# A diffusion transformer block on one core: scale/K weights in 4+5 tiles, ones in PSUM, early transposes, another LN1 order

## The chip, the cores and the metric

One core of one Trainium2 chip. The metric is the device time of one execution in microseconds (us). In the text PE is TensorE, DVE VectorE, ACT ScalarE, POOL GpSimd and SP SyncE, which issues the weight loads and the output stores. SBUF is the on-chip memory that loads go to, PSUM the one that PE writes its sums to. A DMA "lands" when its data have arrived. The "dense part" is the stretch from the first K matmul on, where PE hardly ever waits.

## The reference, cut to what matters

```python
B, N, D = (2, 256, 1152)                      # F = 4 * D, all bfloat16
mod = (_silu(c) @ w_mod).reshape(B, 6, 1, D)
shift_a, scale_a, gate_a, shift_m, scale_m, gate_m = [mod[:, i] for i in range(6)]
h = _layernorm(x, axis=-1) * (1 + scale_a) + shift_a
qkv = (h @ wqkv).reshape(B, N, 3, H, Dh)      # H = 2
# ... attention, wo, gate, second layernorm, gelu MLP
return x + gate_m * m
```

## The kernel before

D is nine tiles of 128 ("k-tiles"); the 512 tokens are four token tiles, two a batch. The program is a list of units with dependencies; a small list scheduler fixes each engine's order ahead of time, and PE's order is simply the order of the source. K needs only LN(x)·(1+scale), since the shift adds the same vector to every key row's product and is put in for Q and V later. So the kernel loads the scale columns of w_mod and the K weights first and starts K as soon as the first columns are there:

```python
KC = 5                                        # k-tiles in the first scale part
for (ka, kb) in ((0, KC), (KC, KT)):          # loads: scale part, its K weights, next part ...
    for k0 in range(0, KT, 3):                # a part comes in three thirds
        dma(WSC[:, k0:k0 + 3, ka * P:kb * P], wmod_v[:, k0:k0 + 3, D + ka * P:D + kb * P], ...)
    for kt in range(ka, kb):
        dma(WK[:, kt, :], wqkv_v[:, kt, D:2 * D], ...)
for k0 in range(0, KT, 3):                    # then the shift weights
    dma(WSH[:, k0:k0 + 3, :], wmod_v[:, k0:k0 + 3, 0:D], ...)

def ln_stats_act(src, junk, mv_t, msq, rstd_t, tag):      # token tiles 0 and 3
    act(... Square, accum_out=msq ...)
    act(... Identity, scale=1.0 / D, accum_out=mean ...)
    dve(... var = mean * mean - msq ...)
    dve(... var = -var + EPS ...)
    pool(... rstd = var ** -0.5 ...)

def sc1a(ka, kb):                             # 1 + scale, PSUM to SBUF
    dve(... tensor_scalar(out=o, in0=m, scalar1=1.0, op0=ALU.add) ...)

# PE's order
warm(7, "b"); ...                             # warm-up matmuls on zeros
xn_T(1)                                       # transposes of a normalised token tile
# scale sums of k-tiles 0-2, xn_T(0), sums 3-5, warm, sums 6-8, warm
sc1a(0, KC)
for kt in range(KC): hk(kt, 0, ...)           # HK = xn * (1 + scale)
for kt in range(KC):
    for i in range(4): k_pair((kt,), i, 0)    # K, batch 0, two output tiles a pair
    if kt == 1: xn_T(2)
    if kt == 2: xn_T(3)
k_pair(range(KC), 0, 1)                       # K, batch 1
for kt in range(KT): mod_kt(WSC, kt, 0, ..., (KC, KT))   # second scale part, 36 small matmuls
sc1a(KC, KT)
k_pair(range(KC), 1, 1); k_pair(range(KC), 2, 1)         # 20 matmuls hide the copy
# ... rest of K
S.unit("pe", KT * c_mm(CH) + 100.0, "shr")    # "the shift product": reads WSH k-tile by k-tile
# ...
k_pair(range(KT), 3, 1, bank=1)               # the last K pair, 18 matmuls
# ... then Q, attention, V, wo, MLP
```

## Time and profile before

| before | |
|---|---|
| median of 3 runs | 247.52 us (247.26 to 247.64) |
| span of the profiled run | 245.2 us |
| PE busy | 98% |
| last first-part scale third has landed | 10.93 us |
| first K matmul | 12.28 us |
| last PE matmul starts | 242.39 us |
| last store issued | 243.38 us |

The landings are the times at which the last of a DMA's 16 semaphore increments came; the first K matmul is the first one with 256 columns.

First lines of the page of before: the span, PE's and the weight loads' busy time, the share of the 40 slices in which PE was busy, the clock that the throttle granted, and the chain that ended last.

```profile
span 245.2 us, 4025 instructions
PE 240.2 (98%) x1750; PEld 147.6 (60%) x1760; DVE 98.5 (40%) x201; ACT 63.1 (26%) x127; POOL 20.2 (8%) x34
...
PE   7999999999999999999999999999999999999995
...
PEclk9999999999999999999999999999999999999999
...
PE 94%; DMA 3%; SPq 1%; DVE 0%; issue 0%
```

PE is the engine that the time is made of: nearly the whole chain runs through it, at full granted clock. "Busy" in the first slices includes warm-up matmuls that compute nothing, so those slices are not full of work.

The same chain in order of time, of before: start, length, what.

```profile
2.82 8.11 DMA arena<-in_w_mod_dram
10.93 0.05 issue
10.97 0.67 PE psum L687 x15
11.64 0.02 issue
11.66 0.18 DVE arena L788
11.85 0.03 issue
11.87 0.36 DVE arena L797
12.23 0.04 issue
12.28 1.92 PE psum L687 x16
14.20 0.50 PE psum L690 x9
...
16.08 16.11 PE psum L687 x198
```

Read downwards: a scale load, 15 scale sums, "1+" (line 788), the first scaling (line 797), K. From 12.28 us on it is PE alone. The start costs 1.35 us from the landing to K.

PE in order of time around the second scale sums (first line) and around the shift product (second line), of before; a bracket with an idle time would stand at the end of a line if PE had waited.

```profile
16.79 5.46 PE L687 MATMUL psum<-arena 128*128 128x256 bf16 x74
26.77 3.46 PE L687 MATMUL psum<-arena 128*128 128x256 bf16 x51
```

No bracket: PE ran through both places. Taken matmul by matmul there were two short gaps, 0.06 us after the matmul that starts at 17.55 and 0.13 us after that at 18.48.

### The profile page before, as it was taken

What the parts mean: (1) busy time and instruction counts of PE and PEld (TensorE: products, weight loads), DVE (VectorE), ACT (ScalarE), POOL (GpSimd) and SP (SyncE); (2) the same over time, 40 slices, a digit from 0 to 9 for tenths busy, and PEclk for the clock granted to TensorE, in tenths of its full rate; (3) what the DMA queues carried; (4) which work ended last, traced back from release to release, by engine and by line L of the source; (5) the groups of instructions that cost most, each with busy time, mean ns of one, the idle gap of its engine ahead of it and who ended that gap; (6) DMA issues with size and microseconds to landing.
All of it is one profiled execution on the core that took longest, in us unless ns stands there. A gap on an engine that the chain in (4) does not pass through costs nothing.

```text
span 245.2 us, 4025 instructions
## 1 busy us (share of the span) xinstructions
PE 240.2 (98%) x1750; PEld 147.6 (60%) x1760; DVE 98.5 (40%) x201; ACT 63.1 (26%) x127; POOL 20.2 (8%) x34
## 2 busy tenths in 40 slices
PE   7999999999999999999999999999999999999995
PEld 2588754457666766798544444444556655665675
DVE  3743450456312679869999700000012222111112
ACT  5730340244312305983322233222000000000000
POOL 1300000000011166600000000020000000000000
PEclk9999999999999999999999999999999999999999
DMA  6999999999993999969943589003000000000000
GB/s 236 364 377 392 391 390 407 417 422 404 382 305 112 340 387 391 391 211 402 349 122 111 182 268 357 0 3 96 0 16 19 16 16 20 16 16 16 29 22 19
DMA packets 28844, 51.59 MB, mean 210 GB/s; under 512 B 1559, under 2 KB 15643, under 8 KB 28827
## 3 DMA queue, kind: packets, MB, share of 16 engines
q1 hardware_dynamic: 28384, 50.14, 56.7%
q0 software_dynamic: 416, 1.19, 1.5%
q8 instruction: 14, 0.23, 0.4%
q14 instruction: 3, 0.02, 0.0%
q10 hardware_dynamic: 27, 0.00, 0.0%
HBM read 50.14 MB, written 1.19 MB: 209 GB/s over the span
## 4 chain that ended last, share of the span: by engine, by line
PE 94%; DMA 3%; SPq 1%; DVE 0%; issue 0%
PE psum L687 92%; DMA arena<-in_w_mod_dram 3%; PE psum L690 2%; SPq L668 1%; DVE arena L797 0%; DVE arena L1214 0%; DVE arena L1215 0%; DVE arena L788 0%
## 5 line engine op out<-in xcount | busy, mean ns | idle before, releaser
L687 PE MATMUL psum<-arena 128*128 128x384 bf16 (+12 forms) x1661 | 236.7, 310 | 2.4 <-POOL arena L710 1.4
L687 PEld LDWEIGHTS psum<-arena 128*128 128x128 bf16 (+3 forms) x1671 | 142.2, 97 | 92.5 <-issue 4.6
L1214 DVE TENSOR_TENSOR arena<-psum,arena 128x384 f32<-128x384 f32 (+3 forms) x14 | 7.0, 501 | 68.0 <-PE psum L687 68.0
L1124 ACT ACTIVATE arena<-psum 128x512 bf16<-128x512 f32 (+1 forms) x44 | 22.4, 520 | 42.7 <-PE psum L687 42.7
L684 DVE CAST arena<-psum 128x512 bf16<-128x512 f32 (+4 forms) x22 | 13.8, 633 | 31.7 <-PE psum L687 31.6
L682 ACT ACTIVATE arena<-psum 128x512 bf16<-128x512 f32 (+6 forms) x27 | 14.7, 562 | 35.0 <-PE psum L687 32.4
L1025 DVE SCALAR_TENSOR_TENSOR arena<-arena 128x1152 f32<-128x1152 bf16 x16 | 22.7, 1416 | 0.5
L1092 POOL TENSOR_TENSOR arena<-arena 128x384 f32<-128x384 f32 x12 | 10.9, 911 | 14.0 <-DVE arena L1091 11.8
L668 POOL DMA_DIRECT2D dit_scratch<-arena x3 | 1.8, 610 | 116.7 <-ACT arena L682 59.9
L734 DVE BATCH_NORM_STATS2 arena<-arena 128x6 f32<-128x384 f32 (+1 forms) x18 | 9.5, 549 | 0.0
L1037 DVE CAST arena<-psum 72x32 bf16<-72x32 f32 x1 | 0.2, 188 | 21.2 <-PE psum L687 21.2
L1091 DVE TENSOR_TENSOR arena<-psum,arena 128x384 f32<-128x384 f32 x12 | 6.7, 555 | 3.8 <-PE psum L687 3.8
L1097 ACT ACTIVATE arena<-arena 128x1152 bf16<-128x1152 f32 x4 | 5.3, 1344 | 9.8 <-DVE arena L1096 9.8
L690 PEld LDWEIGHTS psum<-arena 128*128 128x128 bf16 (+1 forms) x89 | 5.8, 98 | 2.4 <-DMA arena<-in_c_dram 0.8
L1215 DVE TENSOR_TENSOR arena<-arena 128x384 bf16<-128x384 f32 (+3 forms) x14 | 7.0, 502 | 0.5
L690 PE MATMUL psum<-arena 128*128 128x128 bf16 (+1 forms) x89 | 7.1, 219 | 0.1
L1114 ACT ACTIVATE arena<-psum,arena 128x128 bf16<-128x128 bf16 x16 | 6.1, 455 | 2.8 <-PE psum L690 2.2
L1111 DVE TENSOR_SCALAR arena<-psum,arena 128x128 bf16<-128x128 bf16 x20 | 5.5, 337 | 1.9 <-PE psum L690 1.9
L955 ACT ACTIVATE arena<-psum,arena 128x256 bf16<-128x256 f32 x8 | 3.7, 469 | 7.3 <-DVE arena L952 4.6
L738 POOL TENSOR_TENSOR arena<-arena 128x1 f32<-128x1 f32 x6 | 3.3, 552 | 7.9 <-DVE arena L737 7.9
L951 DVE TENSOR_REDUCE arena<-psum 128x2 f32<-128x512 f32 x4 | 2.8, 692 | 2.6 <-PE psum L687 2.6
L797 DVE TENSOR_SCALAR arena<-psum,arena 128x256 bf16<-128x256 bf16 x7 | 2.4, 349 | 3.6 <-PE psum L690 2.3
(43 smaller groups left out, 42.9 us busy)
## 6 DMA issues: line engine op xcount, KB each, us to landing
arena<-in_w_mod_dram SPq DMA_DIRECT2D x4, 2592.0 KB, 20.2
arena<-in_w_fc_dram SPq DMA_DIRECT2D x9, 1152.0 KB, 7.3
arena<-in_w_fc_dram SPq DMA_DIRECT2D x4, 2592.0 KB, 16.2
arena<-in_wqkv_dram SPq DMA_DIRECT2D x18, 288.0 KB, 9.9
arena<-in_w_mod_dram SPq DMA_DIRECT2D x3, 864.0 KB, 12.5
arena<-in_wqkv_dram SPq DMA_DIRECT2D x1, 2592.0 KB, 12.1
arena<-in_wo_dram SPq DMA_DIRECT2D x1, 2592.0 KB, 32.8
arena<-in_w_mod_dram SPq DMA_DIRECT2D x3, 480.0 KB, 7.5
```

Of the source, the lines that this page charges most:

```text
L682: act(c_act(n), lambda e: e.activation(out=dst, in_=src, func=ACTF.Copy), [src], [dst], name)
L684: dve(c_dve_psum16(n) if psum16 else c_dve_psum32(n), lambda e: e.tensor_copy(dst, src), [src], [dst], name)
L687: S.instr(lambda e: e.matmul(o, lhsT=l, rhs=r, start=st, stop=sp, **kw), reads=[l, r], writes=[o])
L690: S.instr(lambda e: e.transpose(o, i_, idn), reads=[i_, idn], writes=[o])
L734: dve(550, lambda e, s=s, o=o: e.bn_stats(out=o, in_=s), [s], [o], "bn_%s_%d" % (tag, ci))
L1025: dve(1270, lambda e, w=w, s=s, acc=acc: e.scalar_tensor_tensor(out=acc, in0=w, scalar=s, in1=acc, op0=ALU.mult, op1=ALU.add), [w, s, acc] ...
L1091: dve(550, lambda e, o=o, ga=ga, x1c=x1c: e.tensor_tensor(out=x1c, in0=o, in1=ga, op=ALU.mult), [o, ga], [x1c], "wo_t1_%d_%d" % (t, ci))
L1092: S.op("pool", 930, lambda e, xs=xs, x1c=x1c: e.tensor_tensor(out=x1c, in0=x1c, in1=xs, op=ALU.add), reads=[x1c, xs], writes=[x1c], name=" ...
L1114: act(440, lambda e, o=o, dst=dst, s1=s1, s2=s2: e.activation(out=dst, in_=o, func=ACTF.Identity, scale=s1, bias=s2), [o, s1, s2], [dst], ...
L1124: act(c_act(ntok), lambda e: e.activation(out=dst, in_=o, func=ACTF.Gelu_apprx_tanh), [o], [dst], "gelu_%d_%d" % (f, tok0))
L1214: dve(c_dve_psum32(w), lambda e, o=o, gm=gm, t1=t1: e.tensor_tensor(out=t1, in0=o, in1=gm, op=ALU.mult), [o, gm], [t1], "fc2_t1_%d_%d" % ( ...
L1215: dve(c_dve_32(w), lambda e, t1=t1, x1c=x1c, ost=ost: e.tensor_tensor(out=ost, in0=t1, in1=x1c, op=ALU.add), [t1, x1c], [ost], "fc2_out_%d ...
```

## The change

The intent: start K earlier (a smaller first scale part, a shorter chain from its sums to K), put work into the time in which PE waits anyway (transposes of token tile 3), and rearrange what was tight. The core of the diff:

```diff
-KC = 5
+KC = 4
@@ LN1 statistics on ACT (token tiles 0 and 3)
-            act(... Square ...);  act(... Identity, mean ...)
-            dve(... var = mean * mean - msq ...);  dve(... -var + EPS ...)
+            act(... Identity, mean ...)
+            pool(... var = mean * mean - EPS ...)
+            act(... Square ...)
+            (dve if tag == "ln1_3" else pool)(... var = msq - var ...)
             pool(... rstd ...)
@@ scale sums accumulate on ones that a matmul puts into PSUM
-    mm(ps32(7, ...), W[...], ST[...], kt == 0 and f == fs[0], kt == KT - 1, ...)
+    mm(ps32(7, ...), W[...], ST[...], False, kt == KT - 1, ...)
+        def sc_ones(ka, kb):
+            mm(ps32(7, 2 * ka, 2 * (kb - ka)), IDENT, ONES[:, 2 * ka:2 * kb], True, True)
-            dve(170, ... tensor_scalar(out=o, in0=m, scalar1=1.0 ...) ...)
+            dve(180, ... tensor_copy(o, m) ...)
-            dst, s1 = HK[...], SC1A[:, kt * 2 + b:kt * 2 + b + 1]
+            s1 = ps32(7, 0, 1) if kt == 0 and b == 0 else SC1A[:, kt * 2 + b:kt * 2 + b + 1]
@@ PE's order
-        sc1a(0, KC) ... xn_T(2) after K step 1, xn_T(3) after K step 2
+        hk(0, 0); sc1a(0, KC); ...
+        xn_T(3, 0, 8)                 # eight of nine transposes ahead of K
+        k_first(0); k_first(1); xn_T(3, 8, 9); xn_T(2); ...
         k_pair(range(KC), 0, 1)
+        k_pair(range(KC), 1, 1)
+        sc_ones(KC, KT)
         for kt in range(KT):
+            if kt == 6:
+                k_pair(range(2), 2, 1)            # half of a K pair between the sums
             mod_kt(WSC, kt, 0, "scb_%d" % kt, (KC, KT))
         sc1a(KC, KT)
-        k_pair(range(KC), 1, 1); k_pair(range(KC), 2, 1)
+        k_pair(range(2, KC), 2, 1)
+        S.order_after(by["rstd_ln1_2"], by["rstd_ln1_3"])   # tile 3 before tile 2
```

Left out: other PSUM banks for the transposes, other places for the later warm-up matmuls (one fewer in all), which engine does some copies and scalings, the scheduler's cost constants, the fixed orders of DVE and ACT. From the shift product on, every engine's order is what it was.

## The prediction

> **What bounds the kernel.** TensorE's instruction stream. The page has PE busy 98% of 245.2 us at granted clock 1.0; the chain of waits is 94% PE. Matmul by matmul, in order of time, PE is dense from the first K matmul (12.28 us) to the end: the only gaps are 57 ns (17.55), 129 ns (18.48) and fixed ones of about 0.1 us. So the time is "start of K" plus a nearly fixed sum; busy time before 12.28 us is mostly warm-up. The start is set by loads and a short chain: the last scale third lands at 10.93 us (DMA landings; the queues move some 390 GB/s without pause), its 15 small matmuls end about 11.52, "1+" runs 11.66-11.83, the first scaling starts at 11.87 (351 ns), K at 12.28.
>
> **What the change does.**
> 1. Scale columns in 4 then 5 tiles: each first third is 393 KB, not 492. Thirds of 393 KB landed 1.1 us apart in before, those of 492 KB 1.25. I expect the last at 10.3-10.5 us, and three fewer small matmuls (80 ns).
> 2. Ones put into PSUM by a matmul, first scaling reading its scalar from PSUM: the 0.2 us copy leaves the path.
> 3. Eight transposes of batch 1 (56 ns each, 0.45 us) go from the dense part into PE's waiting time. But K now queues behind them, and they behind the LN1 of tile 3.
> 4. LN1: sum before square, one variance step after it, tile 3 before tile 2: one DVE step (0.2 us) less in each chain. I expect tile 3 normalised at about 10.6-11.2 us, K at 11.5-11.7. POOL's power step took 818 ns while DVE normalised, 547-567 otherwise; this agrees with the Trainium skill, "SBUF — State Buffer", Who interferes with whom (an exclusive shared port), and may eat some of it.
> 5. The second scale part has 45 small matmuls, not 36 (+0.24 us, dense part), and only four K matmuls (0.44 us) after it to hide drain, copy and scaling (about 0.9 us in before, hidden by 20 matmuls). I expect a new stall of 0.3-0.5 us near 19 us.
>
> Sum when PE reaches the shift product (28.285 us before): 0.6-0.7 earlier start, +0.2 net work, +0.2 old stalls gone, -0.3 to -0.5 new stall: 0.4-0.7 us ahead.
>
> **What caps it.** That product needs the shift weights, whose last third lands at 28.62 us in before, while PE needs it at about 29.26: slack 0.64 us. The bytes ahead of it don't change, so it should land at the same time; any lead over 0.64 us becomes a wait there. Later weights have microseconds of slack (query weights land from 29.4, used from 34.2). The later order on every engine is unchanged.
>
> **Prediction:** 247.0 us, 8 in 10 between 246.4 and 247.7. Faster by over 2%: 0.01; within 2%: 0.98; slower: 0.01.
>
> **What would show it.** K's first matmul at 11.4-11.8 us; transposes of tile 3 ending just before; a PE gap of 0.3-0.5 us after the second scale sums; the shift product starting at 27.6-27.9 with little wait on its weights (over 0.3 us says the cap binds); from 32 us on, PE unchanged and shifted.
>
> **What would make it wrong.** Tile 3's LN1 late; bank conflicts (batch 1 now shares banks with batch 0's copies and the scale sums) stalling PE; a slow DMA engine delaying one third (one straggled by 0.75 us in before); less warm-up lowering the clock; or the shift weights landing earlier.

## More of the kernel before

SP issues the output stores in order, and ahead of the very last one it waits for all but the last two to have landed:

```python
if ins is last_out:
    for o in outs[:-2]:
        eng_handle.wait_ge(dma_sems[o.dma_sem], o.dma_val)
```

The waits of SP's queue, of before: who waited for whom, us in total, times, longest.

```profile
SPq L668 <- PE psum L687: 107.5, 21, 17.7
SPq L668 <- DVE arena L1215: 95.8, 13, 37.2
SPq L485 <- DMA out_dram<-arena: 1.1, 1, 1.1
```

Line 485 is the final wait for the last store. The wait ahead of the last store (line 471) does not appear: it had been met when SP came to it.

## The result

| | before | changed |
|---|---|---|
| median | 247.52 us (247.26 to 247.64, 4 runs) | 247.66 us (247.23 to 247.96, 4 runs) |
| ratio | | 1.0005 (0.9985 to 1.0026) |

The change made no difference that these runs resolve. That is the predicted class and inside the predicted range, near its upper edge. The forecast was 0.5 us faster, so the question is where half a microsecond went.

First the start, of the changed kernel, in order of time (PE and DVE lines of this stretch; some others are left out):

```profile
10.70 0.47 PE L687 MATMUL psum<-arena 128*128 128x2 bf16 x12 [0.21 <-DMA arena<-in_w_mod_dram]
11.03 0.61 PE L690 MATMUL psum<-arena 128*128 128x128 bf16 x8
11.29 0.36 DVE L800 TENSOR_SCALAR arena<-psum 128x256 bf16<-128x256 bf16 x1 [0.47 <-PE psum L690]
11.57 0.16 DVE L790 COPY arena<-psum 128x8 f32<-128x8 f32 x1
11.71 0.94 PE L687 MATMUL psum<-arena 128*128 128x256 bf16 x7
```

The last first-part scale third landed at 10.65 us. Twelve sums, eight early transposes (line 690), the first scaling (line 800), K at 11.71 us: 1.05 us from the landing, and the copy (line 790) now comes after the first scaling. The scaling's bracket names the transposes as what released it; whether they hold it is tested in a_both_tback_tail.

The chain that ended last, of the changed kernel, in order of time:

```profile
14.77 14.32 DMA arena<-in_w_mod_dram
29.10 0.04 issue
29.14 30.90 PE psum L687 x195
```

In before the chain left the loads for good at 10.93 us. Now it stays with a load of w_mod until 29.10 us: the shift weights.

PE in order of time around the second scale sums (first two lines) and around the shift product (last two), of the changed kernel; the bracket is the idle time before the line and what ended it.

```profile
16.75 3.02 PE L687 MATMUL psum<-arena 128*128 128x256 bf16 x61
20.04 2.14 PE L687 MATMUL psum<-arena 128*128 128x256 bf16 x18 [0.27 <-DVE arena L800]
...
26.81 2.10 PE L687 MATMUL psum<-arena 128*128 128x256 bf16 x32
29.14 1.08 PE L687 MATMUL psum<-arena 128*2 128x384 bf16 x15 [0.22 <-DMA arena<-in_w_mod_dram]
```

Both brackets are new. The bracket counts from the modelled end of the matmul before; from issue to issue, less the earlier matmul's own columns, the two waits are 0.43 us (for the first scaling of the second part, line 800) and 0.39 us.

The waits of SP's queue, of the changed kernel:

```profile
SPq L668 <- PE psum L687: 105.5, 21, 17.0
SPq L668 <- DVE arena L1234: 95.8, 13, 37.2
SPq L471 <- DMA out_dram<-arena: 1.3, 1, 1.3
SPq L485 <- DMA out_dram<-arena: 1.1, 1, 1.1
```

The third line is new, and the prediction has nothing like it: SP waited 1.3 us for an earlier store before it issued the last one.

A sum that closes, from the two traces (us):

| | before | changed |
|---|---|---|
| first K matmul | 12.28 | 11.71 |
| from it to the start of the last PE matmul | 230.11 | 230.56 |
| from there to the last store's issue | 0.99 | 1.85 |
| last store issued | 243.38 | 244.12 |

The middle row is accounted for: 230.11 - 0.19 (the two old gaps) - 0.18 (eight transposes of 56 ns fewer, nine small matmuls of 27 ns and one with the ones more) + 0.43 + 0.39 = 230.56. So in this pair of traces the start gave 0.57 us, the dense part took 0.45 back, and the tail took 0.86 more.

### The profile page after: what moved, and what is told of

Its sections match the earlier page's. It is cut to its first block, busy times and chain, and to the rows that moved or that the text cites. A ratio compares the mean times of both kernels' runs of the same rounds, so it can differ in the third digit from the quotient of the medians.

```text
span 246.0 us, 4040 instructions
## 1 busy us (share of the span) xinstructions
PE 240.3 (98%) x1761; PEld 147.6 (60%) x1761; DVE 97.9 (40%) x199; ACT 63.2 (26%) x126; POOL 21.1 (9%) x37
## 4 chain that ended last, share of the span: by engine, by line
PE 87%; DMA 6%; SPq 5%; issue 0%; DVE 0%
PE psum L687 86%; DMA arena<-in_w_mod_dram 6%; SPq L668 5%; PE psum L690 1%; DVE arena L1233 0%; DVE arena L1234 0%
## 5 line engine op out<-in xcount | busy, mean ns | idle before, releaser
L687 PE MATMUL psum<-arena 128*128 128x384 bf16 (+9 forms) x1672 | 237.1, 310 | 2.2 <-POOL arena L710 1.4
L687 PEld LDWEIGHTS psum<-arena 128*128 128x128 bf16 (+2 forms) x1672 | 142.4, 97 | 92.7 <-issue 4.6
L682 ACT ACTIVATE arena<-psum 128x512 bf16<-128x512 f32 (+6 forms) x27 | 15.2, 578 | 38.5 <-PE psum L687 34.6
L927 ACT ACTIVATE arena<-arena 128x256 bf16<-128x256 bf16 x6 | 2.5, 496 | 4.2 <-DVE arena L921 4.2
## 6 DMA issues: line engine op xcount, KB each, us to landing
arena<-in_w_mod_dram SPq DMA_DIRECT2D x3, 480.0 KB, 10.3
```

The source lines that it names most:

```text
L682: act(c_act(n), lambda e: e.activation(out=dst, in_=src, func=ACTF.Copy), [src], [dst], name)
L687: S.instr(lambda e: e.matmul(o, lhsT=l, rhs=r, start=st, stop=sp, **kw), reads=[l, r], writes=[o])
```

## The experiments

Two waits and a late store are read from single traces here. In the experiments the "tail edit" stands for moving SP's wait for the third last store behind the last issue:

```diff
-                        for o in outs[:-2]:
+                        for o in outs[:-3]:
...
-                for o in outs[-2:-1]:
+                for o in outs[-3:-1]:
```

Every store is still waited for before the program ends, and all kernels below gave correct results. Runs of one group shared a chip and the runs of before: in the first group before had a median of 247.22 us (11 runs), in the second 247.24 (11), in the third 247.19 (9).

### Group 1: the tail and the cap

**a_again**: the changed kernel, not edited.

> The changed kernel again, nothing edited, as the control of this group and for a second trace. Theory: PE is 0.5 us ahead when it reaches the shift product, waits there 0.3 to 0.5 us for the last third of the shift weights, and ends 0.1 us ahead of before; the last output store is sometimes held 0.7 us, because it waits for an earlier store that shared a DMA engine with a 16 KB instruction fetch. So the runs fall into two groups near 247.3 and 247.9. Rival (the changed kernel is simply equal): runs spread evenly around 247.6 and the second trace shows no store that is late by over 1 us.

Measured: 247.59 us median, ratio 1.0013 (1.0001 to 1.0025). Its runs were 247.02, 247.23, 247.59, 247.59, 247.67 and 247.94; with the four above, two clumps are suggested but not clean. The interval lies just above 1: in this group the changed kernel was, if anything, slower than before, by about 0.1%. The profiled run was the fastest, 247.02 us: its store was not late, K started at 11.81, the wait in the shift product was 0.11 us. So neither the late store nor the size of that wait is the same in each execution.

**a_tail**: the changed kernel with the tail edit.

> The changed kernel, whose last output store no longer waits for the third last one (that wait moves behind the last issue). Theory of the late store: the slow group goes; all runs within 247.0 to 247.5, median about 247.25, that is 0.3 to 0.5 us under the control, and in the trace the last store is issued within 0.3 us of the vector engine's last instruction. Rival (the tail does not matter, the spread is elsewhere): as the control, 247.6 with the same spread.

Measured: 247.13 us median (246.95 to 247.17), ratio 0.9995 (0.9983 to 1.0008). The runs over 247.2 us are gone: a half microsecond less at the median than the unedited kernel on the same chip, as the late-store theory wants. The last store was issued 0.99 us after the last PE matmul's start.

**b_tail**: before with the tail edit.

> The kernel before with the same edit of the last store's wait. Theory: its fetch started at 242.23 us, after the store had landed, so it has little to gain: 247.3 to 247.5, at most 0.15 us better than before. The changed kernel with the edit should then be 0.1 to 0.2 us faster than this one (what PE is ahead after the wait for the shift weights). Rival (the wait costs both alike): before gains the same 0.3 to 0.5 us.

Measured: 247.01 us median (246.89 to 247.51), ratio 0.9999 (0.9987 to 1.0011). Nothing by the ratio; by the median 0.2 us, a little more than the 0.15 that the expectation allowed, and below its range of times, as before itself was in this group. Against it the changed kernel with the edit is 0.12 us slower by the median and 0.07 us faster by the mean (247.09 to 247.16): with the tail out of the way, the 0.1 to 0.2 us that had been expected do not show.

**a_shlate_tail**: the changed kernel with the tail edit, and part of the last K pair moved ahead of the shift product.

```diff
+        k_pair(range(5), 3, 1, bank=1)            # ten matmuls, 1.09 us
         S.unit("pe", KT * c_mm(CH) + 100.0, "shr")
...
-        k_pair(range(KT), 3, 1, bank=1)
+        k_pair(range(5, KT), 3, 1, bank=1)
```

> The changed kernel with the tail edit, and ten of the 18 matmuls of the K pair that follow the shift product moved in front of it (1.09 us of work), so that the shift weights have landed when PE asks for them. Theory of the cap: PE's wait of 0.39 us inside the shift product goes, the next work moves up by it, and the time falls 0.3 to 0.45 us under the changed kernel with the tail edit alone: about 246.85. Rival (PE was not held by those weights, or the wait comes back at a later load): same time as with the tail edit alone, within 0.1 us.

Measured: 246.89 us median (246.78 to 247.14), ratio 0.9990 (0.9978 to 1.0002). PE in order of time around the shift product, of this kernel:

```profile
26.75 3.52 PE L687 MATMUL psum<-arena 128*128 128x256 bf16 x51
```

The bracket of the changed kernel is gone, and from the first K matmul to the last PE matmul it is 230.18 us, against 230.58 in the trace of a_tail, which had 0.41 us of wait there: the moved work hid the wait whole. The time fell by 0.24 us at the median, somewhat under the 0.3 to 0.45 expected, and the runs of the two kernels overlap. One reason stands in this trace: K started late, at 11.97 us, although its scale weights were early (9.86 us): PE's warm-up matmuls reached full speed only at 7.6 us, and the first transposes began at 8.6 us behind them (7.8 us in the changed kernel's trace).

The same trace shows the late store without its cost: the third last store landed at 243.83 us, 1.7 us after its fifteen other increments, and the last store went out at 243.14 all the same.

### Group 2: the gap after the scale sums, the early transposes, the late store made on purpose

**a_nosplit_tail**: the changed kernel with the tail edit and the sums whole again.

```diff
-            if kt == 6:
-                k_pair(range(2), 2, 1)
...
-        k_pair(range(2, KC), 2, 1)
+        k_pair(range(KC), 2, 1)
```

> The changed kernel with the tail edit, and its last item undone: the last scale sums stand ahead of the whole K pair again, so eight K matmuls (0.87 us) follow them and not four. The shift product stays where it is. Theory (the shift weights cap the lead): the PE gap of 0.43 us after the scale sums shrinks under 0.1 us, PE's wait inside the shift product grows by as much (to 0.5 to 0.9 us), and the time stays within 0.15 us of the changed kernel with the tail edit alone (247.13 in the group before). Rival (the gap is a loss of its own): 0.4 us faster.

Measured: 247.21 us median (246.59 to 247.72), ratio 0.9997 (0.9985 to 1.0010). The time is as expected (0.08 us over a_tail, in another group). The details missed: the gap shrank to 0.23 us only, so draining, copying and scaling take about 1.1 us here and not 0.87. The difference is in the drain: the copy began 0.57 us after the last sum had started, with 45 sums in a row before it, and 0.34 us after it where the half pair left only 15 in a row (0.50 us after the 36 of before). And the wait in the shift product was 0.18 us. In this trace K had started at 12.17 us, so PE came to the shift product late and had little to wait for. The trace therefore does not show the gap turning into that wait; only the time says that closing half of it bought nothing.

**a_both_tail**: sums whole, and ten K matmuls ahead of the shift product.

> Both edits on top of the tail edit: sums ahead of the whole pair, and ten K matmuls moved ahead of the shift product. Theory: now the closed gap is worth its 0.43 us, because nothing waits for it downstream: the wait in the shift product is under 0.15 us, PE reaches the query product 0.7 to 0.9 us earlier relative to its first K matmul than in the changed kernel, and the time is 246.4 to 246.6, some 0.3 to 0.45 under the shift edit alone and 0.5 to 0.7 under the sums edit alone. Rival (a later load or engine caps it too): no better than 246.85.

Measured: 246.99 us median (246.85 to 247.05), ratio 0.9989 (0.9976 to 1.0002). This missed: no better than moving the K matmuls alone. PE in order of time around the scale sums, of this kernel:

```profile
16.77 1.73 PE L687 MATMUL psum<-arena 128*128 128x256 bf16 x38
18.84 3.41 PE L687 MATMUL psum<-arena 128*128 128x2 bf16 x41 [0.34 <-DMA arena<-in_w_mod_dram]
```

The gap after the sums is gone, and a wait of 0.48 us (issue to issue) stands inside them: the last third of the second scale part landed at 18.79 us, and without the half pair in between PE asked for it at 18.36. So the half pair between the sums has a use: it covers a late third. With only four k-tiles done by then, there seem to be too few K matmuls to cover both the load before the sums and the chain after them; no run tried another split.

**a_both_tback_tail**: as a_both_tail, the eight early transposes back behind the second K step.

```diff
-        xn_T(3, 0, 8)
...
-        xn_T(3, 8, 9)
+        xn_T(3)
```

> As the one with both edits, but the eight early transposes of batch 1 stand behind the second K step again. Theory as predicted blind: K starts no more than 0.1 us earlier or later (the first scaling, not the transposes, releases it), 0.45 us of transposes are back in the dense part, the time is 0.35 to 0.5 us longer than with both edits. Rival (early transposes hold K back by what they save): equal within 0.15 us.

Measured: 247.23 us median (246.38 to 247.54), ratio 0.9996 (0.9983 to 1.0010), 0.24 us over a_both_tail. K started 1.09 us after its scale weights had landed, with early transposes 1.05: they do not hold K back. From K to the last PE matmul it is 230.43 us; that of a_both_tail, less its wait of 0.48, plus this one's gap of 0.23, plus 0.45 of transposes, is 230.23 - 0.48 + 0.23 + 0.45 = 230.43. The expected 0.35 to 0.5 us are there in the sum; this trace lacked the other's wait for the scale third, which is why the time shows half.

**b_fetch**: before with 14 tiny matmuls in PE's idle time; the tail not edited.

```diff
+        for i in range(14):
+            S.unit("pe", 27.0, "tiny_%d" % i)
+            mm(ps32(5, 0, 2), IDENT, Q4B[:, 0:2], True, True)
         S.unit("pe", 100, "c_T")
```

> The kernel before, with 14 matmuls of two columns added in PE's idle time ahead of the transpose of c (0.38 us of work in 0.84 us of idle), its last store waiting as it did. They change no result; they bring each later instruction fetch forward by 28 instructions, so the last fetch should begin about 0.4 us earlier against PE's end than in before, among the packets of the third last store. Theory of the late store: that store's last piece lands 0.7 to 1.5 us late in some or most runs, the last store is issued that much later, and the time grows by 0.4 to 0.8 us in those runs. Rival (the late store belongs to the change, or is chance): as before, within 0.15 us.

Measured: 247.99 us median (247.72 to 248.38), ratio 1.0032 (1.0020 to 1.0044): all five runs slower than the slowest of the eleven runs of before beside them (247.69). In the profiled run PE itself was early: K started at 11.86 us, and the last PE matmul at 242.06. The waits of SP's queue, of this kernel:

```profile
SPq L471 <- DMA out_dram<-arena: 1.4, 1, 1.4
SPq L485 <- DMA out_dram<-arena: 1.1, 1, 1.1
```

The changed kernel's line 471 has appeared in the kernel before. What these kernels show at the end (us; the fetch is the last 16 KB packet of the instruction queue, the increments are those of the third last store):

| trace | fetch | 15th increment | 16th increment | last store issued |
|---|---|---|---|---|
| before | 242.23 to 243.16 | 242.37 | 242.40 | 243.38 |
| changed | 241.93 to 242.97 | 242.28 | 243.98 | 244.12 |
| a_again | 241.79 to 243.08 | 242.08 | 242.11 | 243.09 |
| a_shlate_tail | 241.77 to 242.78 | 242.16 | 243.83 | 243.14 (did not wait) |
| b_fetch | 241.79 to 242.74 | 242.08 | 243.79 | 243.93 |

Fifteen of sixteen increments come in time and one comes 1.7 us late, about a microsecond after the fetch has ended. That fits a fetch that takes one DMA engine for a microsecond and gets in ahead of that engine's piece of the store; it is an inference from the times. In none of the nine other traces, where the fetch began at most 0.1 us before the store's first increment or after it, was a piece late; within some 0.2 us before it, the start alone does not tell: those of the changed kernel, of a_shlate_tail and of b_fetch began 0.17, 0.22 and 0.11 us before and did harm, that of a_again 0.15 us before and did none. The trace does not name the DMA engine, each kernel has one trace only, and b_fetch with the tail edit, which should win the time back, was not run. Earlier fetches moved as meant: the last but one began at 224.8 us, against 227.3 and 227.4 in b_tail and before. For the last one the shift by the 14 matmuls was smaller than I had expected: the fetch came 0.27 us ahead of the last PE matmul, against 0.16 and 0.11 ahead and 0.22 behind in three traces of before and its variants with the tail edit.

### Group 3: controls, and a candidate

**b_shlate_tail**: before with the tail edit and the ten moved K matmuls.

> The kernel before with the tail edit and the ten K matmuls moved ahead of the shift product: the control for the cap. Theory: before never waited there (slack 0.64 us in its first trace), so nothing is won: within 0.1 us of before with the tail edit alone (247.0 to 247.1), and K's first matmul to PE's last stays at 230.1 us. It also gives one more trace of before's start: I expect K's first matmul between 11.8 and 12.3 us, as in the three traces at hand (12.28, 12.07, 11.86). Rival (moving it helps by itself): 0.2 to 0.4 us faster.

Measured: 247.29 us median (247.04 to 247.38), ratio 1.0002 (0.9990 to 1.0015), and 230.11 us from K to the last PE matmul. Moving the matmuls wins nothing where there was no wait. The time is 0.28 us over b_tail's median (another group), where at most 0.1 had been expected; K started at 12.35 us, just outside what I had expected and 0.28 us after b_tail's.

**a_loadsb_tail**: the changed kernel with the tail edit and the loads of before.

```diff
-        for (ka, kb) in ((0, KC), (KC, KT)):
+        for (ka, kb) in ((0, 5), (5, KT)):
```

> The changed kernel with the tail edit, its computing in 4 and 5 tiles as it is, but its loads in the sizes and order of before (scale columns in 5 and 4 tiles, five K tiles between). Theory: in seven traces of the changed load order the last third of the shift weights landed at 28.9 to 29.6 us, in three of before's at 28.6 to 28.9, because thirds with rows of 1 KB at the start run slower. With the loads of before it lands 28.5 to 28.9, the wait in the shift product is under 0.2 us, the last first-part scale third lands 0.2 to 0.3 us later than in the changed kernel, and the two nearly cancel: 247.0 to 247.2. Rival (the later landing is chance): landing at 28.9 to 29.3 all the same, and the time 0.2 us or more over the changed kernel with the tail edit.

Measured: 247.19 us median (246.72 to 247.43), ratio 1.0004 (0.9990 to 1.0017). The last third of the shift weights landed at 28.86 us and the wait in the shift product was nil; K to the last PE matmul took 230.21 us, as in kernels that hide that wait. The last first-part scale third landed at 10.77 us, 0.15 us later than the mean of the changed order (0.2 to 0.3 expected). The landing of the shift weights is what the theory said, in one trace; the time did not move.

**a_shlate_tail_warm4**: a_shlate_tail with three warm-up matmuls fewer.

```diff
-        warm(7, "b")
+        warm(4, "b")
```

> The changed kernel with the tail edit, the moved shift product, and three of the first warm-up matmuls dropped: the best candidate. PE runs a matmul of 512 columns in 427 ns at first and in 216 ns later; the traces so far changed over at 4.6 to 7.6 us, whatever the kernel, and where it came late the warm-up matmuls themselves delayed the first transposes (8.45 us and not 7.8) and K. Theory: with three fewer the transposes are not held, K starts at 11.6 to 11.8 us, and the time is 0 to 0.2 us under the same kernel with seven (246.89). Rival (fewer warm-ups make the change-over later): K starts later than 12.0 us and the time grows by 0.2 us or more.

Measured: 246.79 us median (246.73 to 247.42), ratio 0.9988 (0.9976 to 1.0001). The lowest median of all, 0.4 us under before at the median, but one of its five runs was at 247.42 and the interval just touches 1. K started at 11.80 us. PE's change to full speed came at 6.3 us here (in a_again, with seven warm-ups, at 4.6 us), so the case for which the matmuls were dropped (a late change, 7.6 us in a_shlate_tail) did not occur, and the theory of the warm-up stays untested.

## Why the prediction was right or wrong

With all thirteen traces, the terms of the predicted sum can be measured on more than one pair. "Loads of before" are four traces of before's kernels (and a_loadsb_tail where only loads matter), "changed loads" the other eight.

| term | predicted | measured |
|---|---|---|
| last first-part scale third | 10.3 to 10.5 us | mean 10.62 (9.86 to 11.12); loads of before: mean 10.75 (10.36 to 10.99) |
| landing to K | about 1.2 us, from 1.35 | 1.05 to 1.15, one trace 2.11, from 1.35 to 1.50 |
| first K matmul | 11.5 to 11.7, from 12.28 | mean 11.83 (11.62 to 12.17), from a mean of 12.14 (11.86 to 12.35) |
| net work and old gaps (time less) | -0.2 and -0.2 | -0.18 and -0.19 |
| gap after the second sums | 0.3 to 0.5 us | 0.43 in every trace with the split sums |
| shift product starts | 27.6 to 27.9 | 27.78, 27.87, 27.89 |
| shift weights landed | as before, 28.62 | mean 29.17; loads of before: mean 28.77 |
| tail | not in the prediction | 0.86 us more in some runs |

**Right, mechanism and size.** The chain from the landing to K (it gave 0.3 us, the sum had 0.15), the transposes in the waiting time (a_both_tback_tail: K is not held, and 0.45 us return when they move back), the new gap and its size, the place where the lead would be taken back. In the first trace K at 11.71 us and the shift product at 27.78 us were at the edge of the ranges or inside. POOL's power step, which the prediction named as a risk, ran as the Trainium skill, "SBUF — State Buffer", Who interferes with whom, has it (DVE and POOL share ports exclusively): 787 and 684 ns beside a normalising DVE, 549 and 569 ns without one, in the changed kernel's trace.

**Right in mechanism, wrong in size: the earlier start.** "0.6-0.7 earlier start" measured 0.31 us as a mean, and the two sets of traces overlap. In seven of the eight traces the chain gave 0.3 us; the landing gave 0.13 as a mean where I had put about 0.5, and nearly all of that is one trace (a_shlate_tail, 9.86 us), whose K did not follow. Without it the landing gave 0.02 us. There are two reasons. The thirds that I took as 1.1 us apart came 1.22 us apart on the leading engine at the start of the changed kernel (5.41 to 9.06 us for three, in its first trace), because the 1.1 had been measured later in the program. And 12.28 us for K in before was one trace; three more traces of before's kernels gave 11.86, 12.07 and 12.35.

**Wrong in one point: "the bytes ahead of it don't change, so it should land at the same time".** The shift weights landed 0.40 us later in the changed order (29.17 against 28.77), 0.17 us of it already on the first DMA engine to finish (26.79 against 26.62), the rest because the slowest of the 16 lagged more. The slack that I had put at 0.64 us was therefore smaller, and PE waited 0.11, 0.39 and 0.41 us in the three traces with the order of the changed kernel (0.18 us in a_nosplit_tail). That this wait is real is shown by a_shlate_tail against a_tail (230.18 and 230.58 us from K to the end of PE), and b_shlate_tail, where the same edit wins nothing, shows that before as it stands has no such wait. The wait is not the changed kernel's alone, though: in b_fetch PE came as early (27.86 us), the weights landed at 28.89, and it waited 0.10 us. That the load order makes the later landing rests on one trace of a_loadsb_tail (28.86) beside eight of the other order (28.92 to 29.58). The leading engine's pace agrees: a first-part third took 1.22 to 1.28 us (393 KB) in the changed order and 1.36 to 1.38 us (492 KB) in that of before, a second-part third 1.34 to 1.36 us (492 KB) and 1.11 to 1.13 us (393 KB), with a_loadsb_tail on before's side. Three of each make about 7.8 and 7.5 us for the same bytes. Why the smaller thirds are slow at the start and not later, no run shows.

**Missing: the tail.** The prediction took everything from 32 us on as "unchanged and shifted". It was, on PE. But a last store that waits for an earlier one makes the end depend on the slowest of 16 DMA engines, and one of them was 1.7 us late; an instruction fetch in the same tenths of a microsecond is the likely cause. In the two traces of the unedited changed kernel that fetch came 0.31 and 0.34 us ahead of PE's last matmul, in that of before 0.16. By the times of the runs, a_tail takes the cost out of the changed kernel; b_fetch puts it into the kernel before without any part of the change. Whether the change moved the fetch, and with which instructions, is not settled: a_tail, whose PE order is the changed kernel's, had it 0.19 us ahead.

The time fell inside the range of 246.4 to 247.7 partly by luck. All three errors went the same way, the measured 247.66 us is near the edge, and the 0.5 us that the sum promised did not come; "within 2%" was nearly certain for a change this small.

So the expected half microsecond went to three places: about 0.3 us of it was never there (the start), 0.1 to 0.4 us turned into a wait for the shift weights, and in the runs with a late store another 0.7 to 0.9 us was added at the end (0.75 us by b_fetch's median, 0.86 in the changed kernel's trace). What is left open: single runs of any of these kernels still differ by 0.3 us and more, and a difference of 0.2 us between two medians here is not clear of that. No version was shown faster than before outside its interval; the best is a_shlate_tail_warm4 at 0.9988 (0.9976 to 1.0001).

## What to carry to other kernels

When the time is a start plus a dense stream on one engine, write it as a sum that closes (start, stream, tail) and measure each term on several traces before forecasting a gain of the same size as their spread. A lead won at the start lasts until the next load with too little slack: find that place first and move independent work ahead of it. A wait that is free in one trace, such as one for an earlier store ahead of the last, can be decided by a tenth of a microsecond elsewhere; put it behind the last issue, where it cost nothing in a_shlate_tail.

## What the Trainium skill lacked or had wrong

- "Runtime: NRT & Kernel Launch", Instruction fetch mechanics, says that instructions come in blocks of 16 KiB over a DMA queue of the sequencer's own and that the cost of a block boundary is "mostly hidden". The blocks are in these traces (14 packets of 16,384 bytes, 0.9 to 1.5 us each). Neither this page nor "DMA: Bandwidth & Descriptors" says how much a fetch can cost a data transfer: in three traces one of a store's 16 pieces came 1.7 us late beside a fetch (the fetch as cause is inferred), and with a wait behind it the kernel lost 0.8 us at the median (b_fetch, ratio 1.0032).
- "DMA: Bandwidth & Descriptors", Why a DMA increments its semaphore by 16 and not by 1, says that up to 16 DMA engines finish independently. The traces agree, and the size is worth adding: between the first and the 16th increment of the last shift load lay 2.0 to 2.7 us in every trace, so the leading engine's pace is a poor forecast of a landing.
- "TensorE: Matmul & The Clock Gate", What you observe, gives the change to full speed around 4 us into sustained matmuls, ±500 ns from run to run. Here warm-up matmuls of 512 columns began at 1.41 us and the change (427 to 216 ns a matmul) came at 4.6 to 7.6 us, which is 3.2 to 6.2 us after the first; the page explains the variation by a free-running window, but the spread of 3 us here is wider than its ±500 ns. PE was idle for part of the 0.3 us around its first transpose, near 3.6 us, so the activity was not wholly sustained. The profile's PEclk row showed full clock all the time, so this is better seen in the pace of the matmuls; the trace's own clock records begin only at the change (6.15 us in before).
